# Turning the pack-attention weights in 32x32 blocks and through DRAM, from the third batch on

## The chip, the cores and the metric

The kernel runs on one core of a Trainium2 chip. The metric is device time in microseconds (us): 712.52 median of 3 runs (712.44 to 712.74). TensorE (PE) multiplies matrices into PSUM, its operands stand in SBUF; VectorE (DVE), ScalarE (ACT) and GpSimd (POOL) do elementwise work; SyncE (SP) issues nearly all DMA transfers. Each engine runs its own instructions in order and waits on semaphores for the others.

## The reference

Eight batches, each of 8 heads, 576 tokens, head width 64. For every batch and head a packed query set `p` (32 rows) attends to `k` and `v`; its result P serves as keys and values for `q`. The result, 4608 tokens by 512, goes through a feed-forward layer.

```python
p_packed = sm_attn(p, k, v)               # softmax(p k^T / 8) v : 32 x 64 per head
out = sm_attn(q, p_packed, p_packed)      # 576 x 64 per head
x = out.transpose(0, 2, 1, 3).reshape(B * S, H * D)
h = x @ w_in                              # 512 -> 2048
g = h * sigmoid(1.702 * h)
return g @ w_out                          # 2048 -> 512
```

Everything is float32. The two large products are made from pairs of rounded float32 parts (`hi` and `lo`), three products each.

## The kernel before, in words

For a batch `b` the second attention and `w_in` are folded together: M = P w_in (`m_chunk`, four column chunks of 512, parts `mhi` and `mlo` made by `m_upper` and `m_lower`), then h = A M (`h_mm`, 16 row blocks f of 128 by two token halves, 6 matmuls each), the gate (`h_tanh` on ACT, `h_gate` and `h_over` on DVE), its two parts (`h_upper`, `h_lower`), and the product with `w_out` (`out_mm`, 3 matmuls for each block f and each of four token groups, summed over f in four PSUM banks). The 64 tokens that don't fill a group of 128 are kept for two batches together and multiplied by `over_mm`.

The attention of batch b+1 is made in the middle of the feed-forward of batch b. Its first part: `scores1_mm` (two token halves; four heads of one parity stand in the 128 partitions, 32 rows of `p` each), `scores1_copy`, `scores1_max`, `bias1`, `exp1` (exponentials of one parity `eo`, a tile `x1` of 128x576), `sum1`. Then the weights have to be turned so that tokens are in the partitions: `turn1_mm` transposes four 128x128 pieces of `x1` on TensorE against the identity `ident` (line 340), once for each parity; `turn1_copy` brings the bank to the SBUF tile `aT` (lines 116, 118); `turn1_last_mm` and `turn1_last_copy` (lines 351, 359, 361) do the last 64 tokens, with a mask that zeroes the 64 that were done already. `pack` (line 373, 80 small matmuls) multiplies `aT` with `v`; `pack_end`, `pack_turn_mm`, `scores2_mm` and the second softmax (`max2` to `a_lower`) follow.

The order of all the work is written out by hand: `order` is a list of steps, run once, and each engine's instructions come in the order in which the list issues them. There is no other scheduler: what stands ahead in the list on the same engine goes first. Tiles with the same tag share buffers in turn: tag `x` has 5 (each `x1`, `x2`, `xt` takes one), `kqv` has 2 for all of k, q and v, tags `mhi`/`mlo` have 2 (`MB`). DMA instructions stand in the list too (`load`, `store`, `over_store`) and go out on SP's queue in that order; a DMA that has to wait holds up those behind it.

Of the kernel before, what the change touches and what calls it, by code (L numbers as in the profile page):

```python
# [21 lines left out]
def kernel(  # L22
# [635 lines left out]
    def over_store(pair, k):  # L658
        at = (2 * pair + k + 1) * S - REST
        nc.sync.dma_start(out[at : at + REST, :], taken["over"][k * REST : (k + 1) * REST, :])  # L660
# [123 lines left out]
        (h_gate, 0, 15, 0), (h_gate, 0, 15, 1), (h_over, 0, 15), (turn2, 1, 1), (out_mm, 0, 13, 3),
        (out_mm, 0, 14, 3), (out_mm, 0, 13, 2), (out_mm, 0, 14, 2), (a_upper, 1, 0, None),
        (a_lower, 1, 0, dve), (h_mm, 1, 0, 0), (h_upper, 0, 15, 0), (out_mm, 0, 13, 0),
        (upper_w, 31), (lower_w, 31, dve), (a_upper, 1, 1, None), (a_lower, 1, 1),
# [21 lines left out]
        (h_lower, 1, 2, 1), (out_mm, 1, 2, 2), (h_mm, 1, 5, 0), (out_mm, 1, 3, 2),
        (h_tanh, 1, 5, 0), (h_gate, 1, 5, 0), (out_mm, 1, 2, 0), (m_chunk, 1, 2),  # L810
        (m_upper, 1, 2, 1, None), (scores1_mm, 2, 1, inner), (scores1_max, 2, 1, 1),
        (scores1_max, 2, 1, 0), (bias1, 2, 0), (h_upper, 1, 4, 1, dve), (h_lower, 1, 4, 1, dve),
        (bias1, 2, 1), (scores1_copy, 2, 1, 0), (out_mm, 1, 2, 3), (exp1, 2, 0), (sum1, 2, 0),
        (out_mm, 1, 3, 1), (m_upper, 1, 2, 0, None), (m_lower, 1, 2, 0), (h_upper, 1, 5, 0, dve),
# [10 lines left out]
        (load, "q", 2, 1), (h_lower, 1, 7, 1), (h_lower, 1, 6, 1), (sum1, 2, 1), (out_mm, 1, 6, 1),
        (out_mm, 1, 6, 2), (h_over, 1, 6), (out_mm, 1, 5, 0), (h_mm, 1, 8, 0), (h_tanh, 1, 8, 0),
        (h_gate, 1, 8, 0), (h_upper, 1, 8, 0), (h_lower, 1, 8, 0), (h_mm, 1, 8, 1),
        (h_tanh, 1, 8, 1), (h_over, 1, 8), (store, 0, 2), (h_gate, 1, 8, 1), (h_upper, 1, 8, 1),
        (h_lower, 1, 8, 1), (turn1_copy, 2, 0), (out_mm, 1, 6, 3), (out_mm, 1, 7, 3),
        (out_mm, 1, 6, 0), (h_lower, 1, 7, 0, dve), (h_mm, 1, 10, 0), (out_mm, 1, 7, 0),  # L830
        (h_tanh, 1, 10, 0), (out_mm, 1, 8, 3), (turn1_last_mm, 2), (turn1_last_copy, 2),
        (h_mm, 1, 9, 0), (pack, 2), (h_tanh, 1, 9, 0), (out_mm, 1, 7, 1), (out_mm, 1, 8, 1),
        (pack_end, 2), (h_gate, 1, 10, 0), (h_gate, 1, 9, 0), (h_upper, 1, 9, 0, dve),
        (pack_turn_mm, 2), (out_mm, 1, 7, 2), (pack_turn_copy, 2), (scores2_mm, 2, 0, inner),
        (scores2_turn, 2, 0, 0), (m_chunk, 1, 3), (scores2_turn, 2, 0, 1),
        (h_upper, 1, 10, 0, dve), (max2, 2, 0), (m_upper, 1, 3, 0, None, dve), (h_mm, 1, 10, 1),
# [6 lines left out]
        (out_mm, 1, 9, 3), (m_upper, 1, 3, 1, None), (m_lower, 1, 3, 1), (h_upper, 1, 10, 1),
        (h_upper, 1, 11, 0, dve), (out_mm, 1, 9, 2), (h_lower, 1, 10, 1), (out_mm, 1, 10, 3),
        (h_tanh, 1, 11, 1), (sum2, 2, 0), (h_gate, 1, 11, 1), (h_upper, 1, 11, 1),
        (h_lower, 1, 11, 0), (out_mm, 1, 11, 1), (h_mm, 1, 12, 0), (h_over, 1, 11),
        (h_tanh, 1, 12, 0), (h_mm, 1, 12, 1), (h_tanh, 1, 12, 1), (h_gate, 1, 12, 0),
# [538 lines left out]
```

## Time and profile before

| what | value |
|---|---|
| median of 3 runs | 712.52 us (712.44 to 712.74) |
| the profiled execution | 712.61 us, span 710.8 us |
| PE busy | 697.2 us, 98% |
| DVE, ACT, POOL busy | 404.7, 277.6, 144.6 us |
| `pst` transposes (line 340) | 64 |
| `pstl` transposes (line 351) | 16 |

The span is the time from the first to the last instruction of the profiled execution; the 1.8 us between 710.8 and 712.61 lie around it. Busy times of matmuls overlap (a matmul is 0.3 to 0.6 us long from its start to its end, and the next starts before that), so what a matmul costs TensorE is read from a stretch of them: its length by the number of matmuls in it.

### The profile page before, as it was taken

Reading aid. Unit: us, or ns where it says so; the run is one execution under the profiler, and the core shown is the slowest. Engines: PE = TensorE matmul, PEld = TensorE weight load, DVE = VectorE, ACT = ScalarE, POOL = GpSimd, SP = SyncE. Lnnn points to the kernel's source line nnn. Section 1 sums busy time; section 2 is a strip of 40 time slices with the busy share of each in tenths; the row PEclk is TensorE's granted clock in tenths of the full one; section 3 lists DMA queues with packets and bytes.
Section 4 is the critical chain, followed back from the end, with each engine's and each line's share of the span. In section 5 each row is a group of like instructions: output and inputs, shape, how many; then the busy total and the mean of one; then the engine's idle time right before and its main releaser. Section 6 shows DMA issues by size and latency. Waiting matters only on the chain.

```text
span 710.8 us, 12972 instructions
## 1 busy us (share of the span) xinstructions
PE 697.2 (98%) x5092; PEld 568.2 (80%) x5092; DVE 404.7 (57%) x1027; ACT 277.6 (39%) x668; POOL 144.6 (20%) x172
## 2 busy tenths in 40 slices
PE   7899999999999999999999999999999999999997
PEld 5677788788888888888787788878787887878885
DVE  3988885437563466335635457643774556855543
ACT  4778544423323344454322433332342343333330
POOL 1553342123502223222332212202100000000000
PEclk9999999999999999999999999999999999999999
DMA  9886503310213103021110500313111020010001
GB/s 342 321 328 226 191 1 137 96 39 1 89 41 98 38 22 141 28 85 53 60 60 1 167 1 1 104 34 121 34 63 45 4 88 1 0 60 1 1 16 59
DMA packets 17404, 56.92 MB, mean 80 GB/s; under 512 B 1984, under 2 KB 3008, under 8 KB 16320
## 3 DMA queue, kind: packets, MB, share of 16 engines
q1 hardware_dynamic: 17344, 56.10, 22.2%
q8 instruction: 40, 0.66, 0.4%
q14 instruction: 20, 0.16, 0.1%
HBM read 46.65 MB, written 9.44 MB: 79 GB/s over the span
## 4 chain that ended last, share of the span: by engine, by line
PE 94%; DVE 3%; ACT 1%; DMA 1%; issue 0%; POOL 0%; SPq 0%; DVEq 0%; ACTq 0%; POOLq 0%
PE acc L624 49%; PE h L564 28%; PE acc_over L624 6%; PE psm_None L402 4%; PE ps L247 1%; PE ps L454 1%; PE pspv L373 1%; PE pst L340 1%; DMA k<-pk 1%; DVE x L465 0%; PE warm L124 0%; DVE w_in L217 0%; DVE wo L229 0%; ACT top L205 0%; DVE mx L485 0%
## 5 line engine op out<-in xcount | busy, mean ns | idle before, releaser
L624 PE MATMUL acc<-wo,ghi 128*128 128x512 f32 x1024 | 324.1, 398 | 0.0
L624 PEld LDWEIGHTS acc<-wo,ghi 128*128 128x128 f32 x1024 | 179.6, 188 | 39.0 <-issue 12.8
L624 PE MATMUL acc<-wo,glo 128*128 128x512 f32 x512 | 202.6, 396 | 0.3 <-POOL glo L551 0.2
L572 ACT ACTIVATE g<-h 128x288 f32<-128x288 f32 x256 | 103.9, 410 | 239.9 <-PE h L564 225.0
L554 DVE SCALAR_TENSOR_TENSOR g<-g,h 128x288 f32<-128x288 f32 (+1 forms) x256 | 105.7, 417 | 153.8 <-ACT g L572 152.8
L551 POOL TENSOR_TENSOR glo<-g,ghi 128x288 fp32r<-128x288 f32 (+1 forms) x119 | 89.7, 764 | 309.6 <-ACT ghi L116 199.9
L564 PE MATMUL h<-ahi,mhi 128*128 128x288 f32 x512 | 145.8, 300 | 1.1 <-DVE g L554 0.6
L564 PE MATMUL h<-ahi,mlo 128*128 128x288 f32 x512 | 143.5, 295 | 0.0
L624 PEld LDWEIGHTS acc<-wo,glo 128*128 128x128 f32 x512 | 96.2, 188 | 24.5 <-POOL glo L551 1.6
L564 PEld LDWEIGHTS h<-ahi,mhi 128*128 128x128 f32 x512 | 96.3, 188 | 19.9 <-DVE x L465 5.4
L564 PE MATMUL h<-alo,mhi 128*128 128x288 f32 x512 | 108.9, 294 | 0.0
L564 PEld LDWEIGHTS h<-ahi,mlo 128*128 128x128 f32 x512 | 96.5, 188 | 6.8
L116 ACT CAST ghi<-g 128x288 fp32r<-128x288 f32 (+1 forms) x161 | 63.3, 406 | 60.4 <-DVE g L554 39.3
L564 PEld LDWEIGHTS h<-alo,mhi 128*128 128x128 f32 x512 | 82.3, 188 | 0.2 <-POOL alo L533 0.2
L551 DVE TENSOR_TENSOR glo<-g,ghi 128x288 fp32r<-128x288 f32 (+1 forms) x137 | 60.5, 451 | 19.2 <-ACT ghi L116 15.9
L554 DVE SCALAR_TENSOR_TENSOR over<-g,h 128x64 f32<-128x64 f32 x128 | 27.4, 216 | 35.1 <-ACT g L572 34.8
L430 DVE TENSOR_TENSOR mlo<-psm_None,mhi 128x512 fp32r<-128x512 f32 x62 | 42.2, 684 | 5.9 <-ACT mhi L116 5.5
L624 PE MATMUL acc_over<-wo,ghi_over 128*128 128x512 f32 x128 | 39.9, 392 | 0.0
L116 ACT CAST mhi<-psm_None 128x512 fp32r<-128x512 f32 x44 | 25.7, 586 | 33.3 <-PE psm_None L402 33.3
L402 PE MATMUL psm_None<-w_in,PT 64*32 64x512 f32 x496 | 34.3, 596 | 0.0
L118 DVE CAST ghi<-g 128x224 fp32r<-128x224 f32 (+1 forms) x95 | 30.2, 324 | 5.6 <-PE acc L624 2.4
L624 PEld LDWEIGHTS acc_over<-wo,ghi_over 128*128 128x128 f32 x128 | 23.7, 188 | 4.8
(88 smaller groups left out, 492.9 us busy)
## 6 DMA issues: line engine op xcount, KB each, us to landing
q<-q SPq DMA_DIRECT2D x16, 576.0 KB, 5.6
v<-v SPq DMA_DIRECT2D x8, 1024.0 KB, 5.5
o<-o SPq DMA_DIRECT2D x32, 256.0 KB, 2.4
raw<-w_out SPq DMA_DIRECT2D x16, 511.8 KB, 7.4
raw<-w_in SPq DMA_DIRECT2D x12, 511.8 KB, 9.1
k<-pk SPq DMA_DIRECT2D x8, 640.0 KB, 4.0
k<-pk SPq DMA_DIRECT2D x8, 576.0 KB, 5.3
v<-v_last SPq DMA_DIRECT2D x8, 256.0 KB, 6.2
```

Of the source, the lines that this page charges most:

```text
L116: nc.scalar.copy(dst, src)
L118: engine.tensor_copy(dst, src)
L247: nc.tensor.matmul(bank[32 * j : 32 * j + 32, :NH], kq["p", b][rows(eo), j, :], kq["k", b][rows(eo), half, j, :], start=True, stop=True,)
L340: nc.tensor.transpose(bank[:, cs], st["x", 1, b, eo][:, cs], ident)
L373: nc.tensor.matmul(bank[32 * j : 32 * j + 32, e * D : (e + 1) * D], aT[:, c, e, 32 * j : 32 * j + 32], vt[:, c, e0 : e0 + D], start=(c == ...
L402: nc.tensor.matmul(banks[eo][32 * j : 32 * j + 32, columns(part)], PT[rows(eo), j, :], w_in_sb[fc][rows(eo), j, columns(part)], start=True ...
L430: nc.vector.tensor_tensor(lo, bank[:, at], hi.bitcast(F32), op=ALU.subtract)
L551: engine.tensor_tensor(lo, src, hi.bitcast(F32), op=ALU.subtract)
L554: nc.vector.scalar_tensor_tensor(dst, th, 1.0, h, op0=ALU.add, op1=ALU.mult)
L564: nc.tensor.matmul(h[:, :NH], m[eo][part][:, fo : fo + P], a[:, eo * NH : (eo + 1) * NH], start=(n == 0), stop=(n == len(terms) - 1),)
L572: nc.scalar.activation(g, st["h", b, f, half][:, :NH], AF.Tanh, scale=1.702)
L624: nc.tensor.matmul(acc, gp[:, at : at + P], wo[f][:, part, :], start=(start and i == 0), stop=(stop and i == 2),)
```

## The change

Batches 0 and 1 keep the old way. From batch 2 on, `turn1_mm`, `turn1_copy`, `turn1_last_mm` and `turn1_last_copy` are gone from the list: 12, 12, 6 and 6 steps. For each of these six batches there are instead 2 `turn1_blocks` (one VectorE transpose by 32x32 blocks, SBUF to SBUF, into a tile of tag `x`), 8 `turn1_out` (32 partitions of that tile to a DRAM tile `aside`, in runs of 32 floats) and 6 `turn1_in` (from DRAM to 32 partitions of `aT`, in runs of 256 floats). `aT` becomes one tile that stays, so the rows that the mask zeroed in batch 1 stay zero. Chunk 2 of M in the last batch gets a place of its own, in the buffer that `tops` had at the start. The last `over_store` is issued from ACT. The list is written anew from about the end of batch 0; apart from the steps named, the same steps stand in it, some of the elementwise ones on another engine.

```diff
+    LATE = [(B - 1, 2)]
-    tops = [cst.tile([P, DM], U32, name=f"top{i}") for i in range(4)]
+    tops = wk.tile([P, 4, DM], U32, tag="late", name="tops")
+    tops = [tops[:, i, :] for i in range(4)]
+    aT = cst.tile([P, KC, 2, P], F32, name="aT")
     def turn1_mm(b, eo):
-        if eo == 0:
-            st["aT", b] = wk.tile([P, KC, 2, P], F32, tag="aT", name=f"aT_{b}")
...
+    dram = ctx.enter_context(tc.tile_pool(name="dram", bufs=1, space=bass.MemoryType.DRAM))
+    NQ = P // NPK
+
+    def turn1_blocks(b, eo):
+        st["b", b, eo] = t = x_tile(f"xb_{b}_{eo}")
+        nc.vector.transpose(t, st["x", 1, b, eo])
+
+    def turn1_out(b, eo, j):
+
+        if ("aside", b) not in st:
+            st["aside", b] = dram.tile([NPK, S // NPK * 2 * P], F32, name=f"aside_{b}")
+        d = st["aside", b].rearrange("t (g i n) -> t g i n", i=2 * NP, n=NPK)
+        src = st["b", b, eo][NPK * j : NPK * (j + 1), :]
+        nc.sync.dma_start(d[:, :, NP * eo + j, :], src.rearrange("t (g n) -> t g n", n=NPK))
+
+    def turn1_in(b, i):
+
+        d = st["aside", b].rearrange("t (g i) -> t g i", i=2 * P)
+        n = (KC - 1) * NQ
+        if i < NQ:
+            at, c, src = NPK * i, slice(0, KC - 1), d[:, i:n:NQ, :]
+        else:
+            g = n + i - NQ
+            at, c, src = P - KLAST + NPK * (i - NQ), slice(KC - 1, KC), d[:, g : g + 1, :]
+        dst = aT[at : at + NPK, c].rearrange("t c e n -> t c (e n)")
+        nc.sync.dma_start(dst, src)
...
     def m_upper(b, fc, eo, part=None, engine=nc.scalar):
-        if not part:
+        if not part and (b, fc) in LATE:
+            if ("late", b, fc) not in st:
+                st["late", b, fc] = wk.tile(
+                    [P, 2, 2, FC], F32R, tag="late", name=f"late_{b}_{fc}"
+                )
+            st["m", b, fc, eo] = [st["late", b, fc][:, eo, i, :] for i in range(2)]
+        elif not part:
...
-    def over_store(pair, k):
+    def over_store(pair, k, engine=nc.sync):
```

The list around the new steps of batch 3, and its end:

```diff
+        (scores1_mm, 3, 1, inner), (scores1_copy, 3, 1, 0), (out_mm, 2, 3, 1), (out_mm, 2, 4, 1),
+        (m_upper, 2, 2, 0, None), (h_upper, 2, 4, 1), (out_mm, 2, 5, 1), (scores1_max, 3, 1, 0),
+        (bias1, 3, 0), (scores1_max, 3, 1, 1), (h_lower, 2, 5, 1, dve), (m_lower, 2, 2, 0),
+        (bias1, 3, 1), (exp1, 3, 0), (h_mm, 2, 6, 1), (turn1_blocks, 3, 0), (turn1_out, 3, 0, 0),
+        (scores1_copy, 3, 1, 1), (h_mm, 2, 6, 0), (h_lower, 2, 4, 1), (out_mm, 2, 3, 3),
+        (out_mm, 2, 4, 3), (turn1_out, 3, 0, 2), (exp1, 3, 1), (turn1_blocks, 3, 1),
+        (out_mm, 2, 4, 2), (h_tanh, 2, 6, 0), (turn1_out, 3, 1, 2), (h_tanh, 2, 6, 1),
+        (h_over, 2, 6), (h_gate, 2, 6, 0), (h_upper, 2, 6, 0), (h_lower, 2, 6, 0),
+        (turn1_out, 3, 1, 0), (turn1_out, 3, 0, 3), (turn1_out, 3, 1, 1), (h_gate, 2, 6, 1),
+        (h_upper, 2, 6, 1, dve), (h_lower, 2, 6, 1), (turn1_out, 3, 0, 1), (turn1_out, 3, 1, 3),
+        (h_mm, 2, 7, 0), (out_mm, 2, 5, 2), (h_tanh, 2, 7, 0), (h_gate, 2, 7, 0), (turn1_in, 3, 0),
+        (h_upper, 2, 7, 0), (m_upper, 2, 2, 1, None, dve), (turn1_in, 3, 2), (turn1_in, 3, 1),
+        (turn1_in, 3, 3), (h_mm, 2, 7, 1), (h_tanh, 2, 7, 1), (sum1, 3, 1), (h_gate, 2, 7, 1),
+        (out_mm, 2, 5, 3), (out_mm, 2, 6, 3), (h_upper, 2, 7, 1), (out_mm, 2, 6, 1),
+        (m_lower, 2, 2, 1), (h_mm, 2, 8, 0), (turn1_in, 3, 5), (out_mm, 2, 5, 0),
+        (out_mm, 2, 6, 0), (h_tanh, 2, 8, 0), (h_gate, 2, 8, 0), (turn1_in, 3, 4), (h_over, 2, 7),
+        (sum1, 3, 0), (h_lower, 2, 7, 1), (out_mm, 2, 7, 3), (h_lower, 2, 7, 0), (out_mm, 2, 7, 1),
+        (h_mm, 2, 8, 1), (h_tanh, 2, 8, 1), (h_gate, 2, 8, 1), (out_mm, 2, 7, 0), (h_over, 2, 8),
+        (pack, 3), (pack_end, 3), (h_upper, 2, 8, 0), (h_lower, 2, 8, 0, dve), (h_upper, 2, 8, 1),
...
+        (over_take, 3, dve), (over_store, 3, 1), (over_store, 3, 0, act),
```

## Rows read from the trace of the kernel before

**Rows 1.** The page: busy time by engine, 40 slices, DMA packets.
```profile
PE 697.2 (98%) x5092; PEld 568.2 (80%) x5092; DVE 404.7 (57%) x1027; ACT 277.6 (39%) x668; POOL 144.6 (20%) x172
PE   7899999999999999999999999999999999999997
PEclk9999999999999999999999999999999999999999
...
DMA packets 17404, 56.92 MB, mean 80 GB/s; under 512 B 1984, under 2 KB 3008, under 8 KB 16320
```

**Rows 2.** Busy time in four stretches: length, PE, PEld, DVE, ACT, POOL, clock, DMA.
```profile
0.00:28.00 28.00, 21.42 (x253) 15.27 (x259) 16.30 (x46) 14.29 (x36) 9.64 (x20) 1.00 0.95 368
28.00:128.00 100.00, 98.91 (x739) 79.62 (x730) 75.72 (x173) 62.37 (x141) 39.47 (x38) 1.00 0.46 172
128.00:253.00 125.00, 125.00 (x963) 102.32 (x963) 63.40 (x168) 42.69 (x108) 29.96 (x35) 1.00 0.18 57
253.00:710.80 457.80, 451.88 (x3147) 370.99 (x3145) 249.23 (x642) 158.23 (x385) 65.57 (x80) 1.00 0.14 49
```

**Rows 3.** The chain of waits, 128 to 180 us: start, length, what.
```profile
139.59 0.44 PE pst L340 x4
140.03 2.08 PE acc L624 x9
142.12 0.43 PE pst L340 x4
...
144.63 1.57 PE h L564 x12
...
150.46 0.22 PE pstl L351 x2
...
169.19 1.02 PE psm_None L402 x16
```

**Rows 4.** Groups of instructions by line: count, busy us, mean ns, idle before.
```profile
L116 ACT CAST ghi<-g 128x288 fp32r<-128x288 f32 (+1 forms) x161 | 63.3, 406 | 60.4 <-DVE g L554 39.3 <-PE acc L624 16.8 <-PE acc_over L624 3.2
...
L116 ACT CAST mhi<-psm_None 128x512 fp32r<-128x512 f32 x44 | 25.7, 586 | 33.3 <-PE psm_None L402 33.3
...
L205 ACT CAST top<-raw 128x512 f16<-128x512 bf16 (+1 forms) x36 | 24.5, 717 | 0.7 <-DMA raw<-w_out 0.6 <-DVE dec L217 0.2
...
L510 DVE STREAM_TRANSPOSE xt<-x 128x576 f32<-128x576 f32 (+1 forms) x17 | 12.4, 732 | 1.8 <-POOL x L504 1.7
...
L316 ACT ACTIVATE x<-x,nb 128x576 f32<-128x576 f32 x14 | 10.9, 776 | 3.4 <-DVE nb L300 3.2
L340 PE MATMUL pst<-ident,x 128*128 128x128 f32 x64 | 10.0, 284 | 0.0
...
L116 ACT COPY x<-ps 128x288 f32<-128x288 f32 x21 | 8.3, 399 | 10.9 <-DVE mx L292 7.9 <-PE ps L247 3.0
...
L118 DVE COPY aT<-pst 128x512 f32<-128x512 f32 x4 | 2.7, 687 | 2.6 <-PE pst L340 2.6
...
L316 ACT ACTIVATION_READ_ACCUMULATOR x<-x,nb 128x1 f32 x14 | 2.7, 190 | 0.0
```

**Rows 5.** What TensorE waited for: us, times, longest.
```profile
PE pspv L373 <- ACT aT L359: 0.3, 1, 0.3
```

**Rows 6.** SP's instructions in order of time: start, length, count.
```profile
625.97 1.41 SPq L644 DMA_DIRECT2D o<-o  x3
706.85 1.11 SPq L660 DMA_DIRECT2D o<-o_over  x2
```

**Rows 7.** DMA from 691 to 694 us: packets, share of 16 engines, KB, us to landing.
```profile
q1 hardware_dynamic: 144, 0.26, 23.3%
o<-o SPq DMA_DIRECT2D x1, 256.0 KB, 2.0
```

**Rows 8.** DMA from 240 to 244 us, the same columns.
```profile
q1 hardware_dynamic: 144, 0.66, 51.6%
k<-pk SPq DMA_DIRECT2D x1, 640.0 KB, 3.8
```

**Rows 9.** DMA from 705 to 711 us, the same columns.
```profile
o<-o_over SPq DMA_DIRECT2D x2, 128.0 KB, 2.3
```

**Rows 10.** The chain of waits from 694 us: start, length, what.
```profile
694.95 11.10 PE acc_over L624 x48
...
706.13 0.69 DVE o_over L118
```

More of the change, by code (lines that the diff above doesn't have):

```diff
@@ L784 @@
[L784 to L787, printed above, removed]
+        (h_lower, 0, 14, 1), (h_lower, 0, 13, 1), (out_mm, 0, 12, 1), (exp2, 1, 1),
+        (out_mm, 0, 13, 1), (turn2, 1, 0), (sum2, 1, 1), (norm2, 1, 1, None, pool),
@@ L809 @@
[L809 to L814, printed above, removed]
@@ new lines @@
+        (h_mm, 1, 5, 0), (out_mm, 1, 3, 2), (h_tanh, 1, 5, 0), (h_gate, 1, 5, 0),
+        (out_mm, 1, 2, 0), (m_chunk, 1, 2), (m_upper, 1, 2, 1, None), (scores1_mm, 2, 1, inner),
+        (scores1_max, 2, 1, 1), (scores1_max, 2, 1, 0), (bias1, 2, 0), (h_upper, 1, 4, 1, dve),
+        (h_lower, 1, 4, 1, dve), (bias1, 2, 1), (scores1_copy, 2, 1, 0), (out_mm, 1, 2, 3),
+        (exp1, 2, 0), (turn1_blocks, 2, 0), (sum1, 2, 0), (out_mm, 1, 2, 1), (out_mm, 1, 3, 1),
+        (m_upper, 1, 2, 0, None), (turn1_out, 2, 0, 0), (m_lower, 1, 2, 0), (turn1_out, 2, 0, 1),
@@ L825 @@
[L825 to L836, printed above, removed]
@@ L843 @@
[L843 to L847, printed above, removed]
-        (h_over, 1, 12), (out_mm, 1, 10, 2), (m_chunk, 2, 0), (h_upper, 1, 12, 0),
@@ new lines @@
+        (over_mm, 0, 3), (h_over, 2, 2), (h_gate, 2, 2, 1), (h_lower, 2, 1, 0, dve),
+        (h_mm, 2, 2, 0), (h_tanh, 2, 2, 0), (h_gate, 2, 2, 0), (h_mm, 2, 1, 1), (out_mm, 2, 0, 2),
+        (h_tanh, 2, 1, 1), (h_upper, 2, 2, 0, dve), (h_over, 2, 1), (h_gate, 2, 1, 1),
+        (h_upper, 2, 1, 1), (h_lower, 2, 1, 1), (h_upper, 2, 2, 1, dve), (m_chunk, 2, 1),
+        (m_upper, 2, 1, 0, None), (over_take, 0, dve), (scores1_mm, 3, 0, inner),
+        (h_lower, 2, 2, 1, dve), (scores1_copy, 3, 0, 1, dve), (scores1_max, 3, 0, 1),
@@ new lines @@
+        (out_mm, 4, 2, 1), (out_mm, 4, 2, 2), (scores1_mm, 5, 1, inner), (scores1_max, 5, 1, 0),
+        (scores1_copy, 5, 1, 0), (load, "q", 5, 0), (m_chunk, 4, 2), (h_upper, 4, 4, 1),
+        (bias1, 5, 0), (exp1, 5, 0), (h_mm, 4, 5, 1), (h_upper, 4, 3, 1, dve), (h_lower, 4, 3, 1),
+        (turn1_blocks, 5, 0), (turn1_out, 5, 0, 3), (turn1_out, 5, 0, 2), (h_tanh, 4, 5, 1),
+        (scores1_max, 5, 1, 1), (bias1, 5, 1), (turn1_out, 5, 0, 1), (h_over, 4, 5),
+        (m_upper, 4, 2, 0, None), (m_lower, 4, 2, 0), (scores1_copy, 5, 1, 1), (exp1, 5, 1),
@@ new lines @@
+        (h_gate, 5, 3, 0), (h_mm, 5, 4, 1), (h_upper, 5, 3, 0, dve), (h_lower, 5, 3, 0, dve),
+        (h_tanh, 5, 4, 1), (h_over, 5, 4), (h_gate, 5, 4, 1), (h_upper, 5, 3, 1), (store, 4, 2),
+        (out_mm, 5, 1, 1), (h_lower, 5, 3, 1, dve), (h_mm, 5, 4, 0), (h_tanh, 5, 4, 0),
+        (h_gate, 5, 4, 0), (out_mm, 5, 1, 3), (h_upper, 5, 4, 0, dve), (h_upper, 5, 4, 1, dve),
+        (m_chunk, 5, 2), (m_upper, 5, 2, 1, None), (scores1_mm, 6, 1, inner),
+        (scores1_copy, 6, 1, 1), (scores1_copy, 6, 1, 0, dve), (scores1_max, 6, 1, 0),
@@ new lines @@
+        (turn1_in, 6, 1), (turn1_in, 6, 0), (turn1_in, 6, 3), (turn1_in, 6, 5), (pack, 6),
+        (pack_end, 6), (out_mm, 5, 8, 1), (pack_turn_mm, 6), (pack_turn_copy, 6, dve),
+        (out_mm, 5, 7, 0), (scores2_mm, 6, 0, inner), (scores2_turn, 6, 0, 0), (m_chunk, 5, 3),
+        (m_upper, 5, 3, 0, None), (h_mm, 5, 10, 0), (h_tanh, 5, 10, 0), (m_upper, 5, 3, 1, None),
+        (scores2_turn, 6, 0, 1), (max2, 6, 0), (sub2, 6, 0, None), (h_gate, 5, 10, 0),
+        (h_upper, 5, 10, 0, dve), (h_lower, 5, 10, 0, dve), (h_mm, 5, 9, 1), (h_tanh, 5, 9, 1),
@@ new lines @@
+        (h_lower, 5, 11, 0, dve), (h_upper, 5, 10, 1), (h_lower, 5, 10, 1, dve),
+        (h_gate, 5, 11, 1), (out_mm, 5, 9, 0), (out_mm, 5, 10, 2), (store, 4, 1),
+        (out_mm, 5, 10, 0), (sum2, 6, 0), (m_chunk, 6, 0), (m_upper, 6, 0, 0, None),
+        (load, "k", 7, 0), (scores2_mm, 6, 1, inner), (norm2, 6, 0, None), (out_mm, 5, 10, 3),
+        (scores2_turn, 6, 1, 0), (scores2_turn, 6, 1, 1), (h_mm, 5, 12, 0), (h_tanh, 5, 12, 0),
+        (h_upper, 5, 11, 1, dve), (h_lower, 5, 11, 1, dve), (out_mm, 5, 11, 2), (h_mm, 5, 12, 1),
@@ new lines @@
+        (h_lower, 6, 9, 0, dve), (h_tanh, 6, 9, 1), (h_over, 6, 9), (turn1_in, 7, 0), (pack, 7),
+        (pack_end, 7), (h_mm, 6, 10, 0), (store, 5, 2), (pack_turn_mm, 7), (load, "q", 7, 0),
+        (h_lower, 6, 8, 0, dve), (out_mm, 6, 7, 1), (out_mm, 6, 8, 1), (out_mm, 6, 7, 2),
+        (pack_turn_copy, 7, dve), (h_tanh, 6, 10, 0), (h_gate, 6, 10, 0), (h_gate, 6, 9, 1),
+        (h_upper, 6, 9, 1), (store, 5, 3), (scores2_mm, 7, 0, inner), (m_chunk, 6, 3),
+        (m_upper, 6, 3, 1, None), (scores2_turn, 7, 0, 0), (scores2_turn, 7, 0, 1), (max2, 7, 0),
```

1046 lines of the change are left out of this document (513 added, 533 removed).

## The prediction

> **What bounds the kernel now.** I read the page first: TensorE is busy for 98% of the span at a granted clock of full speed in every slice, which is the higher of its two levels, 2.4 GHz; VectorE stands at 57%, ScalarE at 39% [rows 1]. Then four stretches [rows 2]: from 128 to 253 us TensorE is busy for 125.00 of 125 us, from 253 to the end for 451.88 of 457.8. What is missing there is nearly all the tail: the last matmuls end at 694.95 + 11.10 = 706.05 us [rows 10], 4.75 us before the end, so 5.92 - 4.75 = 1.2 us of real idleness in 458. VectorE is busy for 249/458 = 54% there, the DMA engines for 14%. So from batch 2 on (its first scores come after 100 us) only two things move the end: what TensorE does, and new waits of TensorE. Its waits are small before, those of `pack` for `aT` 0.3 us [rows 5].
>
> **The change part by part**
>
> *Transposes leave TensorE.* The chain shows a group of four at 0.44 and 0.43 us and the two last ones at 0.22 us, with the neighbours at their usual pace on both sides (9 of `out_mm` in 2.08, 12 of `h_mm` in 1.57) [rows 3]. The mean of 284 ns of one [rows 4] counts the overlap and would be too much. Per batch 0.44 + 0.43 + 0.22 = 1.09 us; six batches: **-6.5 us**. Nothing hides them, since TensorE has no idle time there.
>
> *The block transposes.* 12 on VectorE, of the same 128x576 shape as the row at 732 ns [rows 4]: 8.8 us more, less 4 copies of 687 ns. Some 6 us net on an engine with 46% free: 0, hidden beside the matmuls. Behind such a block on VectorE stand gates and parts of g; by both lists the shortest stretch from an `h_mm` to an `out_mm` that uses it is 3 `out_mm` (2.1 us). Without that cover the price would be 12 x 0.73 = 8.8 us. ScalarE loses work only.
>
> *The way through DRAM.* Per batch 8 `turn1_out`, then 6 `turn1_in`, each issued by SP, at 1.41/3 = 0.47 us for one of three in a row [rows 6]. `turn1_in` has to wait until all eight have landed; behind it on SP stand loads of q and k and stores. I went through SP's part of the list: nothing ahead of the new steps waits for work later than `scores1` of the same batch. Of the loads behind them the tightest is the second half of q of batch 4: it now follows both loads of the next k, which wait for `pack`; 9 + 8 + 8 packets of some 0.21 us and 1.7 us of landing are 7 us, with 9.8 us of TensorE work from the end of `pack` to its use. Reuse of the 5 buffers of tag `x` has 17 us or more to spare everywhere. So one deadline counts for each batch: `aT` complete when TensorE comes to `pack`.
>
> For batch 3, the closest, the list has 15 `out_mm` (0.695 us each) and 6 `h_mm` (0.785 us) between the second `scores1_mm` and `pack`: 15.1 us. In that time:
> - ScalarE: copy 0.40, `m_upper` 0.59, `h_upper` 0.41, exp 0.78 + 0.19, copy 0.40, exp 0.97 = 3.7 us; then the second block transpose 0.73, with 0.5 for handing over (an estimate): 5.0 us [rows 4].
> - Six `turn1_out` still to go. One has 32 x 18 = 576 runs of 128 bytes, 36 for each of 16 DMA engines. No row has a run so short. A store of 256 KB has 144 packets in 23.3% of 16 engines in 3 us: 78 ns each [rows 7]; a load with 5 KB packets 51.6% x 16 x 4 / 144 = 229 ns [rows 8]. 2.5 times the bytes take 2.9 times as long, so there is no fixed part to see: by bytes 128 would take 5 ns, and at the other end as long as 2 KB, 78 ns. No row tells which end is nearer; I take the middle of the ratio, 20 ns. One `turn1_out` is then 36 x 20 = 0.72 us of all DMA engines, six 4.3 us (the issue, 0.47 each, hides in it).
> - What landing costs beyond packets: the store landed after 2.0 us, 9 packets an engine of 78 ns in it: 1.3 us [rows 7].
> - Six `turn1_in`: the last is issued 5 x 0.45 = 2.25 us after the first; the 640 KB load landed after 3.8 us, 9 x 229 ns = 2.1 in it, so 1.7 fixed [rows 8], and 8 packets of 1 KB add 0.3: 2.0 us.
>
> Sum: 5.0 + 0.4 + 4.3 + 1.3 + 2.25 + 2.0 = 15.25 against 15.1 us: **+0.1 us**. In the same way for the others, with o for the time of one `turn1_out`, n of them still to go from t on, and 5.95 us for the rest (0.4 + 1.3 + 2.25 + 2.0): a batch can bear o = (work up to `pack` - t - 5.95) / n. Batch 3: (15.1 - 5.0 - 5.95) / 6 = 0.7. Batch 5, with 16 `out_mm`, 5 `h_mm` and an `m_chunk` of 1.0: (16.1 - 5.4 - 5.95) / 5 = 0.95. Batch 4: (18.4 - 4.7 - 5.95) / 6 = 1.3. In 7, 2 and 6 all eight count: (20.3 - 3.6 - 5.95) / 8 = 1.35, (20.2 - 2.6 - 5.95) / 8 = 1.45, (23.1 - 2.8 - 5.95) / 8 = 1.8. Only batch 3 is at its limit with 0.72. At 5 ns no batch waits and the issue bounds: 0 us. At 78 ns, o = 2.8: 12.6 + 9.3 + 9.1 + 11.8 + 10.8 + 8.2 = 62 us of new waits.
>
> The Trainium skill, "DMA: Bandwidth & Descriptors" (section "Specifications"), speaks against this part: transfers need 512 B or more for line rate, and below that the DMA engine reads, modifies and writes. No packet of data in these rows is that small. What it would make of the time is the first rival.
>
> *The tail.* The last two stores are issued in 1.11 us, the second some 0.5 us after the first [rows 6], and each lands after 2.3 us [rows 9]. From ScalarE the second goes beside the first: **-0.5 us** (0 if the issue there is slower by as much). The 0.69 us of `over_take` stays [rows 10].
>
> *A third place for M, `tops` in one tile, the new list.* The third place lets `m_chunk` of the last batch come earlier; TensorE does the same work: 0. The new list can win at most the 1.2 us of idleness and the 1.1 us before 128 us; what it can lose isn't bounded by a row, beyond this: the distances from h to its product, and of the PSUM reuse behind it, are as short and as many as before. I take 0.
>
> Sum against the profiled execution: 712.6 - 6.5 - 0.5 + 0.1 = 705.7; two thirds of the 0.3 us that `pack` waited go as well: **705.5 us**. That execution lies 0.1 us above the median of the runs, less than can be told.
>
> **The rivals**
>
> *Small runs are slow (slower than before).* The mechanism is the one above: each 128-byte run into DRAM costs much more than its bytes. `pack` of every batch then stops TensorE until the last `turn1_in` has landed. It takes back the 7 us at o = 1.38 us, or 38 ns a run: 6 x 0.68 + 5 x 0.43 + 6 x 0.09 + small rests = 7 us. At 50 ns (o = 1.8) the waits sum to 6.5 + 4.3 + 3.1 + 3.7 + 2.7 = 20 us: 726 us; at 78 ns 767. For it: of 17,404 packets only 1984 are under 512 B, 16 for each of the 124 transfers and none of them data [rows 1], so nothing shows the price of a short run. Against it: no fixed part from 2 KB to 5 KB. Chance 0.15. By the rule of the Trainium skill named above a run would be read and written, twice its bytes, 10 ns, and nothing would wait; the page gives no price for it.
>
> *Part is given back.* Two or three `pack`s wait 1 to 2 us each (o near 1.1), or the new list has stops of that sum, or the four parts of `tops`, now one tile, make each of 36 conversions (0.72 us, [rows 4]) wait for the join before it in the first 90 us. 2 to 5 us come back: 708 to 711. For it: SP, the transfers and two engines now stand in a row ahead of `pack`. Chance 0.15.
>
> *Nothing is gained.* If the transposes filled time that TensorE would have waited anyway, for gates or for VectorE, the list would just move the wait: 712. Against it: a full 125 of 125 us [rows 2]. Chance 0.07.
>
> *More is gained*, by the idleness that the new list can take: 704.2. Chance 0.03.
>
> **How the numbers follow.** Forecast 705.5 with its own range 704.6 to 708, chance 0.60. About 0.2% (1.4 us) is what a measurement here can tell from no change. Faster: 0.60 + 0.15 + 0.03 = 0.78. Same: 0.07. Slower: 0.15. The range has the forecast, what is given back and no gain: 704.6 to 713.5; it leaves out some 0.18, the slow runs above and the larger gain below.
>
> **What would show it.** Lines 340 and 351 with 16 and 4 matmuls; TensorE busy about 690 us; the chain still over 94% TensorE. On the row of `pack` the wait for a DMA of `aT`: under 1 us in all by the forecast, over 7 us by the first rival, largest in batch 3. The page's packets under 512 B, 27,648 of them new (48 x 576), with a duration that decides between 5, 20 and 78 ns. The last two stores side by side. Wrong it would be if TensorE waited for something else in sum, VectorE's gates above all, or if a `turn1_out` lands much later than 2.0 us after its issue.

## The result, and the profile after

The changed kernel takes 704.57 us (median of 4, 703.91 to 706.67) against 712.48 before (712.23 to 712.74): ratio 0.9897 with a 95% interval of [0.9885, 0.991] (so in every ratio below), 7.9 us less. The profiled execution took 703.91 us with a span of 702.1; before it was 712.61 and 710.8. Forecast were 705.5 us and a gain of 7.1.

The page of the changed kernel, busy time and slices, answers to [rows 1]:

```profile
PE 688.1 (98%) x5032; PEld 561.8 (80%) x5032; DVE 434.5 (62%) x1099; ACT 259.9 (37%) x621; POOL 121.8 (17%) x141
PE   7899999999999999999999999999999999999997
PEclk9999999999999999999999999999999999999999
DMA packets 49853, 64.01 MB, mean 91 GB/s; under 512 B 30976, under 2 KB 35456, under 8 KB 48768
```

TensorE has exactly 60 matmuls less (5092 - 5032), the 10 transposes of six batches, at the same clock and still at 98%. Packets under 512 B rose by 30,976 - 1984 = 28,992: the 27,648 expected, and 1344 more, 16 for each of the 84 new transfers.

The last two of the four stretches in [rows 2] (length, PE, PEld, DVE, ACT, POOL, clock, DMA):

```profile
128.00:253.00 125.00, 124.08 (x942) 101.94 (x923) 68.23 (x174) 42.50 (x106) 30.03 (x35) 1.00 0.29 82
253.00:702.10 449.10, 443.91 (x3099) 365.40 (x3097) 274.32 (x707) 140.68 (x340) 42.66 (x49) 1.00 0.20 58
```

The stretch that was full before, 128 to 253 us, now lacks 0.92 us; behind it 449.10 - 443.91 = 5.2 us are missing, 4.33 of them the tail behind the last matmul. The groups by line (343 and 354 are the transposes that are left, 374 the block transposes, 406 `pack`; count, busy us, mean ns, idle before) and the list of TensorE's waits (us, times, longest) name it:

```profile
L343 PE MATMUL pst<-ident,x 128*128 128x128 f32 x16 | 2.7, 280 | 0.7 <-ACT x L312 0.7
L354 PE MATMUL pstl<-ident,x 128*128 128x128 f32 x4 | 0.8, 286 | 0.0
L374 DVE STREAM_TRANSPOSE xb<-x 128x576 f32<-128x576 f32 x12 | 9.1, 770 | 5.1 <-ACT x L319 5.0
L406 PE MATMUL pspv<-v,aT 128*32 128x64 f32 x640 | 11.1, 221 | 1.3 <-DMA aT<-aside 0.9 <-ACT aT L362 0.3
```

```profile
PE pspv L406 <- DMA aT<-aside: 0.9, 1, 0.9
PE h L603 <- DVE g L593: 0.6, 1, 0.6
PE acc L663 <- DVE glo L590: 0.5, 1, 0.5
```

One `pack` waits once, and no other does: it is that of batch 3, as the chain of waits from its scores to it shows (start, length, what):

```profile
220.72 0.59 PE ps L250 x16
221.31 0.39 ACT x L117
...
224.27 0.88 ACT x L319 x2
...
225.17 0.78 DVE xb L374
...
228.91 0.63 SPq L382
...
229.58 3.51 DMA aside<-xb
...
234.64 2.76 DMA aT<-aside
...
237.50 1.39 PE pspv L406 x80
```

This is the forecast's row of steps: ScalarE's exp, the second block transpose, SP issuing, the last `turn1_out` landing, SP issuing the `turn1_in`, landing, `pack`. The link that is too long is the 3.51 us of the last `turn1_out`, from its issue to its landing, for which 2.0 were forecast. What one of them costs, from SP's instructions and from DMA in a quiet stretch (batch 7, 559 to 568 us; for a queue packets, MB, share of 16 engines, for an issue KB and us to landing):

```profile
224.89 5.32 SPq L382 DMA_DIRECT2D aside<-xb  x8
```

```profile
q1 hardware_dynamic: 4753, 0.61, 43.4%
aside<-xb SPq DMA_DIRECT2D x8, 72.0 KB, 2.3
```

SP's pitch is 5.32/8 = 0.67 us, and a packet takes 43.4% x 16 x 9 us / 4753 = 13 ns, so a `turn1_out` is 36 x 13 = 0.47 us of the DMA engines: the issue on SP sets the pace, not the transfer.

### The profile page after: what moved, and what is told of

It is laid out like the page before. It is cut to its first block, busy times and chain, and to the rows that moved or that the text cites. A ratio compares the mean times of both kernels' runs of the same rounds, so it can differ in the third digit from the quotient of the medians.

```text
span 702.1 us, 13011 instructions
## 1 busy us (share of the span) xinstructions
PE 688.1 (98%) x5032; PEld 561.8 (80%) x5032; DVE 434.5 (62%) x1099; ACT 259.9 (37%) x621; POOL 121.8 (17%) x141
## 2 busy tenths in 40 slices
DMA packets 49853, 64.01 MB, mean 91 GB/s; under 512 B 30976, under 2 KB 35456, under 8 KB 48768
## 4 chain that ended last, share of the span: by engine, by line
PE 91%; DVE 4%; DMA 2%; issue 1%; ACT 1%; SPq 1%; DVEq 0%; ACTq 0%
PE acc L663 48%; PE h L603 28%; PE acc_over L663 5%; PE psm_None L435 4%; PE ps L493 1%; PE ps L250 1%; PE pspv L406 1%; DMA k<-pk 1%; DMA aside<-xb 0%; DVE mlo L469 0%; DMA aT<-aside 0%; PE warm L125 0%; SPq L382 0%; DVE glo L590 0%; DVE wo L232 0%
## 5 line engine op out<-in xcount | busy, mean ns | idle before, releaser
L603 PE MATMUL h<-ahi,mhi 128*128 128x288 f32 x496 | 140.3, 298 | 1.1 <-DVE g L593 0.6
L603 PE MATMUL h<-ahi,mlo 128*128 128x288 f32 x496 | 138.9, 295 | 0.0
L590 POOL TENSOR_TENSOR glo<-g,ghi 128x288 fp32r<-128x288 f32 (+1 forms) x88 | 67.7, 777 | 243.7 <-ACT ghi L117 115.5
L603 PEld LDWEIGHTS h<-ahi,mhi 128*128 128x128 f32 x496 | 93.2, 188 | 18.9 <-DVE x L504 5.7
L603 PE MATMUL h<-alo,mhi 128*128 128x288 f32 x496 | 105.4, 294 | 0.0
L603 PEld LDWEIGHTS h<-ahi,mlo 128*128 128x128 f32 x496 | 93.3, 188 | 6.9
L590 DVE TENSOR_TENSOR glo<-g,ghi 128x224 fp32r<-128x224 f32 (+1 forms) x168 | 73.9, 452 | 21.0 <-ACT ghi L117 17.5
L603 PEld LDWEIGHTS h<-alo,mhi 128*128 128x128 f32 x496 | 79.6, 188 | 0.2 <-POOL alo L572 0.2
L117 ACT CAST ghi<-g 128x288 fp32r<-128x288 f32 (+1 forms) x135 | 53.2, 405 | 45.8 <-DVE g L593 35.8
L119 DVE CAST ghi<-g 128x288 fp32r<-128x288 f32 (+1 forms) x121 | 36.3, 308 | 6.8 <-PE acc L663 1.4
```

The lines of the kernel that those rows point to most:

```text
L117: nc.scalar.copy(dst, src)
L119: engine.tensor_copy(dst, src)
L590: engine.tensor_tensor(lo, src, hi.bitcast(F32), op=ALU.subtract)
L603: nc.tensor.matmul(h[:, :NH], m[eo][part][:, fo : fo + P], a[:, eo * NH : (eo + 1) * NH], start=(n == 0), stop=(n == len(terms) - 1),)
```

## The experiments

Each has a median of 4 to 11 executions, the kernel before (712.1 to 712.5 us) measured beside it.

**The changed kernel again**, without an edit.

> The changed kernel once more, nothing edited: 704.6 us by both theories. Open is its spread (703.91 to 706.67 in four executions). Theory 1: it is the wait of `pack` of batch 3, of 0.93 us in the one profile seen, where the last `turn1_out` landed 1.3 us later than its neighbours while a 16 KB instruction fetch held one DMA engine; then a new profile shows another wait there (0 to 2 us), and the rest of the gaps of TensorE as before. Rival: the spread lies elsewhere, and the wait of that `pack` is again 0.9.

704.22 us (703.96 to 704.41), ratio 0.9887 [0.9874, 0.9901]. The wait of batch 3's `pack` is the same as in the first profile:

```profile
238.01 1.32 PE L406 MATMUL pspv<-v,aT 128*32 128x64 f32 x80 [0.94 <-DMA aT<-aside]
```

So theory 1 falls: this wait is steady and no cause of spread. The two profiles differ by 0.5 us in the first 28 us, where this one waits 1.0 us for `w_in` and the first didn't. Where 706.67 came from stays open.

**The transposes back on TensorE, in the new list.** For b = 2 to 7:

```
-        (turn1_blocks, b, 0), (turn1_blocks, b, 1),
-        (turn1_out, b, eo, j), (turn1_in, b, i),
+        (turn1_mm, b, 0), (turn1_copy, b, 0),
...
+        (turn1_mm, b, 1), (turn1_copy, b, 1, dve),
...
+        (turn1_last_mm, b), (turn1_last_copy, b),
...
         (pack, b),
```

> The new list with the transposes of batches 2 to 7 back on TensorE (2 x 4 and 2 per batch, 8, 5 and 2 steps of TensorE ahead of `pack`), without block transposes, `turn1_out`, `turn1_in`. The prediction's size of 1.09 us per batch gives 704.6 + 6.5 - 1.0 (the wait of batch 3's `pack` goes) = 710.1 us. The rival size, from the distances between the starts of TensorE's matmuls (0.36 + 0.36 + 0.135 = 0.86 per batch), gives 704.6 + 5.2 - 1.0 = 708.8; then the new list, and not the transposes, gave over 2 us. If the list gave nothing, it is 712.

710.74 us (710.13 to 711.47), ratio 0.998 [0.9971, 0.9989]. That is 6.5 us above the changed kernel, though the wait of batch 3's `pack` is gone. The edit made one wait of its own, for `pn` (0.5 of these; the other 1.1 us is batch 0's and stands in all kernels):

```profile
PE pspt L425 <- ACT pn L419: 1.6, 2, 1.1
```

The transposes are then worth 6.5 + 0.9 - 0.5 = 6.9 us, give or take some 0.6 by the spread of the executions (against the next run, which has neither way, 710.74 - 702.89 - 0.5 = 7.3): the prediction's 6.5 holds, and the rival size of 5.2 doesn't. By the distances between the starts of matmuls the groups themselves take 5.2 us, as the rival has it; but `out_mm`, by the same distances, takes 366.6 us in all here and 364.6 in the next run, so the matmuls around the groups lose 2.0 more. The rest of the way to the old kernel, 712.34 - 710.74 = 1.6 us, is the new list with the tail, without any transposes saved. One wait of the old list that is in no trace of the new one, from the list of waits of the kernel before (the scores of batch 5 wait for a gate, near 374 us):

```profile
PE ps L247 <- DVE g L554: 0.5, 1, 0.5
```

But in sum the waits of TensorE that the traces list behind 28 us are 2.0 us before and 2.1 here, and its idle time ahead of the end of the last matmul is 710.8 - 4.8 - 697.2 = 8.8 us before and 709.1 - 4.4 - 695.7 = 9.0 here. The list's gain is in the busy time, for the same number of matmuls; the page of this run:

```profile
PE 695.7 (98%) x5092; PEld 567.8 (80%) x5092; DVE 430.4 (61%) x1093; ACT 264.9 (37%) x633; POOL 122.0 (17%) x141
```

What makes it shorter stays open. The new list also gives 26 more `h_upper` and 31 more `h_lower` to VectorE, and no run takes that back by itself.

**Without the way through DRAM.**

```
-        (turn1_blocks, b, eo), (turn1_out, b, eo, j), (turn1_in, b, i),
```

> The changed kernel without `turn1_blocks`, `turn1_out` and `turn1_in` in batches 2 to 7 (`pack` there reads the transposed weights of batch 1, so this part of the computation is left out). If the way through DRAM costs TensorE nothing but the wait of batch 3's `pack`: 704.6 - 1.0 = 703.6 us. If the block transposes on VectorE, SP's longer queue or the transfers delay TensorE in other places too: under 703, with the wait of each such place gone from the trace.

702.89 us (702.56 to 703.95), ratio 0.9871 [0.9858, 0.9885], 1.3 us below the changed kernel. 0.9 of it is the wait of `pack`; the waits for g (0.6) and for `glo` (0.5) are those of the changed kernel, so they are the list's. The remaining 0.4 is within what the medians can tell. Twelve block transposes and 84 transfers cost TensorE nothing else.

**The old list with the way through DRAM put in place.** For b = 2 to 7, and `LATE = []`:

```
         (exp1, b, 0),
-        (turn1_mm, b, 0), (turn1_copy, b, 0), (turn1_mm, b, 1), (turn1_copy, b, 1),
-        (turn1_last_mm, b), (turn1_last_copy, b),
+        (turn1_blocks, b, 0), (turn1_out, b, 0, 0), (turn1_out, b, 0, 1),
+        (turn1_out, b, 0, 2), (turn1_out, b, 0, 3),
...
         (exp1, b, 1),
+        (turn1_blocks, b, 1), (turn1_out, b, 1, 0), (turn1_out, b, 1, 1),
+        (turn1_out, b, 1, 2), (turn1_out, b, 1, 3),
+        (turn1_in, b, 0), (turn1_in, b, 1), (turn1_in, b, 2),
+        (turn1_in, b, 3), (turn1_in, b, 4), (turn1_in, b, 5),
```

> The list of before with the way through DRAM put in the place of the transposes: block transpose and four `turn1_out` right behind each `exp1`, six `turn1_in` behind the last; nothing else moved, one place less for M, last store on SP. Theory: from the end of a batch's later exp to `pack` the way needs about 1.0 + 4 x 0.67 + 2.45 + 2.3 + 1.9 = 10 us (pitch of `turn1_out`, landing, six `turn1_in`, landing, as measured in the trace after), and the list of before gives less in batches 3, 4, 5 and 6: waits of 1.0, 1.8, 6.4 and 3.6 us, none in 2 and 7; 712.6 - 5.2 to 6.5 + 12.8 = 719 to 720 us, slower than before. Rival: the order is no matter, since loads and stores on SP have slack: 706 to 707 us with waits under 2 us in all.

728.82 us (725.46 to 729.9), ratio 1.0221 [1.0199, 1.0243]: slower than before. TensorE's waits, its `pack`s of batches 4 and 5, and granted clocks behind them (stretches as above):

```profile
PE pspv L406 <- DMA aT<-aside: 13.3, 4, 4.8
PE h L603 <- DVE g L593: 3.0, 3, 1.6
```

```profile
317.88 1.36 PE L406 MATMUL pspv<-v,aT 128*32 128x64 f32 x80 [2.48 <-DMA aT<-aside]
410.95 2.19 PE L406 MATMUL pspv<-v,aT 128*32 128x64 f32 x80 [4.80 <-DMA aT<-aside]
```

```profile
319.00:322.00 3.00, 3.00 (x22) 2.29 (x11) 0.00 (x0) 0.79 (x3) 0.66 (x1) 0.51 0.52 155
411.00:415.00 4.00, 4.00 (x87) 3.44 (x88) 0.00 (x0) 0.66 (x3) 0.00 (x0) 0.57 0.89 246
500.15:504.15 4.00, 4.00 (x87) 3.63 (x88) 0.00 (x0) 0.53 (x2) 0.00 (x0) 0.60 0.40 121
600.00:604.00 4.00, 3.78 (x103) 2.64 (x111) 0.00 (x0) 0.78 (x3) 0.00 (x0) 1.00 0.21 48
```

The sum of the waits was forecast well (12.8, measured 13.3), their places less so: 2.5, 4.8, 4.3 and 1.8 us in batches 4 to 7, none in 3. The time was missed by 9 us for two reasons that the forecast lacked. Block transposes that stand on VectorE until an exp ends hold up gates behind them: 3.0 us of waits for g instead of 0.6. The first of these, near 230 us, on VectorE:

```profile
228.80 0.78 DVE L374 STREAM_TRANSPOSE xb<-x 128x576 f32<-128x576 f32 x1 [2.00 <-ACT x L319]
```

And behind each of the three longest waits the granted clock is near half, 1.2 GHz, for some microseconds: 0.49 x 3 + 0.43 x 4 + 0.40 x 4 = 4.8 us lost. These make 7.2; some 2 us stay open. So the order is no side matter: the way through DRAM put in the place of the transposes costs 16 us in the old order and wins 6.5 in the new one (710.74 to 704.22). The 7.9 of the whole change have the new list's own gain in them.

**`pack` of batch 3 later.**

```
-        (pack, 3), (pack_end, 3),
...
         (h_mm, 2, 9, 1), (h_tanh, 2, 9, 1), (h_gate, 2, 9, 1), (h_over, 2, 9),
+        (out_mm, 2, 6, 2), (pack, 3), (pack_end, 3),
-        (pack_turn_mm, 3), (pack_turn_copy, 3), (out_mm, 2, 6, 2),
         (h_mm, 2, 9, 0),
...
         (h_lower, 2, 9, 0),
+        (pack_turn_mm, 3), (pack_turn_copy, 3),
```

> The changed kernel with `pack` of batch 3 one `h_mm` and one `out_mm` (0.785 + 0.695 = 1.48 us of TensorE's work) later in the list, everything else in its order. Theory: its wait of 1.0 us for `aT` is the way through DRAM being 1 us too long for the list, and nothing else hangs on it: 704.2 - 1.0 = 703.2 us, no wait of `pack` for a DMA left. Rival: the wait only moves on to `pack_turn` or to the second scores of batch 3, which come after it: 704.2.

703.38 us (702.92 to 703.71), ratio 0.9875 [0.9861, 0.9888]: 0.8 us less, and no wait of `pack` for a DMA in its trace. The wait was TensorE's own loss, and it doesn't come back.

**Long runs instead of short.**

```
-        d = st["aside", b].rearrange("t (g i n) -> t g i n", i=2 * NP, n=NPK)
         src = st["b", b, eo][NPK * j : NPK * (j + 1), :]
-        nc.sync.dma_start(d[:, :, NP * eo + j, :], src.rearrange("t (g n) -> t g n", n=NPK))
+        i = NP * eo + j
+        nc.sync.dma_start(st["aside", b][:, S * i : S * (i + 1)], src)
```

> Each `turn1_out` writes its 32 rows of 2304 bytes as they stand, in one run each, instead of 576 runs of 128 bytes (the order within P's weights is then another, so this part of the result is left out of the computation; bytes, waits and the list are the same). If short runs cost what the trace shows (a pitch of 0.67 us against 0.47 for one issue on SP, 13 ns a packet): the first `turn1_in` of batch 3 is issued some 6 x 0.2 = 1.2 us earlier, the wait of its `pack` is gone, 703.2 us, and no other batch changes. Rival: the wait comes from the landing alone (a 16 KB instruction fetch holds one DMA engine for 1.25 us): pitch and wait stay within 0.3 us of what they were, 704.2.

702.97 us (702.44 to 703.52), ratio 0.9872 [0.9857, 0.9887]; `pack` waits for no DMA. SP in batch 3:

```profile
224.43 3.74 SPq L382 DMA_DIRECT2D aside<-xb  x8
229.14 3.09 SPq L394 DMA_DIRECT2D aT<-aside  x6
```

Eight issues in 3.74 us instead of 5.32, a pitch of 0.47: the first theory has the pitch right. That the wait is gone has more than this one reason. The landing is shorter too (median 1.8 us for the eight, and 1.8 for the last, instead of 3.5), and the first `turn1_in` goes 1.4 us after the last `turn1_out` instead of 3.7, since with this order of bytes it needn't wait for all eight: the waits are not the same, as the expectation has it. So the 704.22 - 702.97 = 1.2 us are the most that 128-byte runs cost the kernel.

**No third place for M.**

```
-    LATE = [(B - 1, 2)]
+    LATE = []
...
-        (m_chunk, 7, 2, inner),
...
         (h_mm, 7, 3, 1), (h_tanh, 7, 3, 1), (h_over, 7, 3),
-        (m_chunk, 7, 3),
+        (m_chunk, 7, 2),
...
         (out_mm, 7, 5, 3),
+        (m_chunk, 7, 3),
```

> The changed kernel without the third place for M: the third `m_chunk` of the last batch and its parts go where the fourth stood (behind the last `h_mm` that reads the first part), the fourth behind the last that reads the second. The prediction took the third place for 0: 704.2 us, within 0.4. Rival: the 2 us that the new list won over the old one beside the transposes come from it: 705.5 or more, with new waits of TensorE between 610 and 650 us.

704.91 us (704.45 to 704.96), ratio 0.9895 [0.9882, 0.9909], 0.7 above the changed kernel. 0.4 of it is a wait for `w_in` in the first 28 us, where nothing was edited (1.4 us against 1.0 in the run above); 0.4 is a second wait for `glo`, near 648 us:

```profile
PE acc L663 <- DVE glo L590: 0.9, 2, 0.5
```

This lies between the two expectations (704.6 and 705.5). By these traces the third place is worth about 0.4 us; it isn't the new list's gain.

**Batch 1 through DRAM as well**, tried twice with `pack` of batch 3 later. In both tries batch 1's `turn1_mm`, `turn1_last_mm` and their copies go, and its second `exp1` moves up. The first time:

```
         (load_w, 21),
+        (turn1_out, 1, 0, 0), (turn1_out, 1, 0, 1), (turn1_out, 1, 0, 2), (turn1_out, 1, 0, 3),
...
         (load_w, 25),
+        (turn1_out, 1, 1, 0), (turn1_out, 1, 1, 1), (turn1_out, 1, 1, 2), (turn1_out, 1, 1, 3),
```

> `pack` of batch 3 later as in the run beside it, and batch 1 through DRAM too (its second exp moved up behind the first; blocks, `turn1_out`, `turn1_in` among the loads of the weights). Theory: 1.09 us of transposes less, and the way fits (from the end of its second exp, now near 56 us, 13 us to `pack` at 69.5): 704.2 - 1.0 - 1.1 = 702.1 us. Rival: in the stage where the weights are still being loaded and decoded, the transfers and the blocks delay the conversions, and TensorE waits for weights or for `aT`: 703.5 or more.

710.0 us (708.41 to 711.78), ratio 0.9969 [0.9956, 0.9981]. The rival: the loads of weights stand on SP behind eight `turn1_out`. The last of those shown goes out at 64.64 us, where with `pack` of batch 3 later alone it is 57.00; ScalarE waits 6.17 us for one, and TensorE 4.0 behind it:

```profile
58.81 2.89 SPq L382 DMA_DIRECT2D aside<-xb  x4
...
64.64 0.38 SPq L189 DMA_DIRECT2D raw<-w_out  x1
```

```profile
70.56 1.39 ACT L208 CAST tops<-raw 128x512 f16<-128x512 bf16 x2 [6.17 <-DMA raw<-w_out]
```

```profile
PE h L603 <- DVE over L593: 4.0, 1, 4.0
PE pspv L406 <- DMA aT<-aside: 1.9, 1, 1.9
```

The waits aren't all of it. Behind each of these two the granted clock is half, 1.2 GHz, while TensorE is at work for 3.04 and 3.80 us (stretches as above), which loses 3.4 us more:

```profile
72.70:75.74 3.04, 3.04 (x9) 2.22 (x9) 2.94 (x4) 3.04 (x8) 2.42 (x2) 0.50 0.99 161
77.60:81.40 3.80, 3.80 (x86) 3.63 (x87) 1.46 (x5) 1.46 (x4) 1.09 (x1) 0.50 0.32 102
```

The second time all eight went behind those loads:

```
         (load, "v", 1, 1),
+        (turn1_out, 1, 0, 0), (turn1_out, 1, 0, 1), (turn1_out, 1, 0, 2), (turn1_out, 1, 0, 3),
+        (turn1_out, 1, 1, 0), (turn1_out, 1, 1, 1), (turn1_out, 1, 1, 2), (turn1_out, 1, 1, 3),
```

> As the run with `pack` of batch 3 later and batch 1 through DRAM, which failed by loads of weights stuck behind eight `turn1_out` on SP (5.1 us on VectorE for a conversion, 4.0 us on TensorE behind it): now the second exp of batch 1 and both block transposes a few steps later, and all `turn1_out` behind the loads of weights and of v, only one load of weights and one of q after them. Theory: SP is free from 58 us on, the last `turn1_out` ends near 63 us, the last `turn1_in` lands near 69, `pack` comes near 69.5: 703.4 - 1.1 (transposes) - 0.3 (its wait for a copy) = 702.0 us. Rival: the way still ends late, or conversions wait again: 703.4 or more.

710.33 us (709.35 to 711.35), ratio 0.9975 [0.9964, 0.9985]. Now `pack` of batch 1 waits 5.9 us, and over the 4 us behind it the granted clock is 0.62. SP between 57 and 72 us:

```profile
57.58 9.09 SPq L382 DMA_DIRECT2D aside<-xb  x8
...
68.37 2.78 SPq L394 DMA_DIRECT2D aT<-aside  x6
```

Behind loads of weights and v the eight take 9.09 us, 1.14 each, not 5.4: the pitch is only 0.67 while the DMA engines have little else. Batch 6 of the changed kernel shows the same: 5.98 us for its last five, while two loads of q and two stores run. So the third batch is the first for which the way through DRAM pays in the orders tried.

**The last store back on SP.**

```
-        (over_store, 3, 0, act),
+        (over_store, 3, 0),
```

> The changed kernel with the second last store back on SP behind the other, nothing else. The prediction's term: 0.5 us longer from the last matmul to the end; by the traces it should be 4.75 us again instead of 4.34, and 704.6 us. Rival: the store from ScalarE is no sooner complete than one queued on SP, and the 0.4 us of difference between the two traces is chance: 4.3 us again, 704.2.

704.57 us (703.62 to 705.03), ratio 0.9894 [0.9879, 0.9909]. From the last matmul's end to the end of the span it is 4.54 us, against 4.33 with ScalarE and 4.76 before. Neither expectation: ScalarE's issue is worth some 0.2 us, and the two traces with SP differ by as much. The changed kernel's last transfers tell why (697 to 702.1 us):

```profile
o<-o_over SPq DMA_DIRECT2D x1, 128.0 KB, 2.3
o<-o_over ACTq DMA_DIRECT2D x1, 128.0 KB, 2.6
```

The half microsecond of queueing is saved, and 0.3 of it goes into a later landing.

**A better version**: `pack` of batch 3 later, and one `out_mm` ahead of each of the two other waits.

```
-        (h_mm, 0, 14, 0), (h_tanh, 0, 14, 0), (h_gate, 0, 14, 0), (out_mm, 0, 12, 2),
+        (out_mm, 0, 12, 2), (h_mm, 0, 14, 0), (h_tanh, 0, 14, 0), (h_gate, 0, 14, 0),
...
+        (out_mm, 2, 14, 2),
         (out_mm, 2, 15, 3),
...
-        (out_mm, 2, 14, 2),
```

> The changed kernel with `pack` of batch 3 later as in the run before, and two `out_mm` moved ahead of the waits of TensorE that the new list left or made: one ahead of the `h_mm` near 94 us that waits for a gate (0.76 us over its usual distance), one ahead of the `out_mm` near 274 us that waits for a part of g (0.68). Theory: such waits are lost time one by one, since nothing but TensorE sets the end: 704.2 - 0.8 - 0.7 - 0.7 = 702.0 us. Rival: each comes back as a wait a few steps on, for the same gate or part of g: 703.4 as with the later `pack` alone.

701.79 us (701.47 to 701.96), ratio 0.985 [0.9837, 0.9864]: faster than both kernels. What TensorE still waits for after 28 us, all of it:

```profile
PE pspv L406 <- ACT aT L362: 0.3, 1, 0.3
PE h L603 <- ACT x L117: 0.2, 1, 0.2
```

## Why the prediction was right, and where it was not

The forecast of 705.5 us lies 0.9 above the measured median and 1.6 above the profiled execution; the median, 704.57, stands at the lower end of the range given (704.6 to 713.5), and the run without an edit at 704.22. By its steps:

- *Transposes, -6.5.* Right: 6.9 by undoing it. Reading the pace from the chain [rows 3] was the right choice.
- *Block transposes on VectorE, 0.* Right: they took 9.1 us (8.8 forecast), and leaving them out with the transfers wins only the wait of `pack` and 0.4 that can't be told from nothing. The cover is the order: put in the old list, they held gates for over 2 us.
- *The way through DRAM, +0.1.* Right in mechanism, place (batch 3 alone) and pitch of `turn1_out` (0.72 forecast, 0.67 measured), mis-sized by 0.8: it cost 0.9. The pitch came out for another reason: a run costs 13 ns, below the 20 chosen, but each issue takes 0.67 on SP, which the forecast had hidden at 0.47. The term that failed is the landing. From the end of the second block transpose to the last `turn1_out` in DRAM were forecast 0.4 + 4.3 + 1.3 = 6.0 us; the chain has 233.09 - 225.95 = 7.1, and 1.5 of the 3.51 us of the last one is more than the 2.0 taken: 0.3 of that is in a landing in a quiet stretch too (2.3), 1.2 is batch 3's alone (see the end). The `turn1_in` came as forecast in sum, 237.41 - 233.09 = 4.3 us against 2.25 + 2.0, though not in parts: by the chain it is the fourth of the six that lets `pack` go, 2.76 us after its issue.
- *The tail, -0.5.* Half right: 0.2 by undoing it, 0.4 between the traces; a later landing on ScalarE's queue takes the rest.
- *Third place for M and the new list, 0.* Wrong: with the transposes on TensorE the new list with the tail is 1.6 us faster than the old one, in spite of a wait of its own of 0.5. Without that wait, and without the 0.2 of the tail, the list is worth 1.9. Some 0.4 is the third place, 0.5 the wait of the scores of batch 5 that is gone; for the other 1 us the record shows no place. The bound of 2.3 us that was given held as a number, but not by its reason: it was put on idle time, and the idle time stayed (8.8 us before, 9.0 with the new list), while the busy time fell.
- *Two thirds of the 0.3 us that `pack` waited.* Wrong: this wait is still there, near 70 us; it is batch 1's, which keeps its transposes.

In the order above the errors are -0.4, 0, +0.8, +0.3, -1.9 and +0.2 us, and they sum to -1.0: 8.1 us were gained against the kernel before beside the run without an edit (712.34 to 704.22), 7.1 forecast. That the number came within a microsecond is partly luck, since the list's error alone is almost twice that. The way and its place, batch 3, are not luck: they were worked out link by link, and the runs show them.

The number that came is that of the rival with the chance 0.03 (more is gained, 704.2), but its mechanism, idle time that the new list takes, is not what the traces show. The first rival (short runs slow) was decided by the packets: 13 ns where it needed 38. The trace of before had a closer row for it than those chosen: its 1984 packets under 512 B, 4 bytes each, take 9 ns (median). The Trainium skill, "DMA: Bandwidth & Descriptors" (section "Specifications"), wants 512 B or more for line rate. The trace agrees: by its share of a 2 KB packet of 78 ns [rows 7] a 128-byte one would take 5 ns, and it takes 13. The second rival (part given back) came in with one `pack` and less than 1 us; nothing of `tops` was seen in the waits.

What the profile was to show came, but for the chain: 91% TensorE where over 94 was forecast, as it follows the way through DRAM for batch 3, and that wait is one microsecond of 700. The sign of being wrong that was named, a `turn1_out` landing much later than 2.0 us, came as well: 3.5 to 4.3 us for the last three of batch 3, and a median of 4.9 for those of batch 6 (466 to 480 us), where there was time to spare and no `pack` waited.

## What to carry to other kernels

When the bounding engine is full, work taken off it pays in full only if the other way ends before the engine arrives, so draw up that way link by link for each place, with the landing of the last transfer taken from a busy stretch: the same substitution lost 16 us in one order and won 6.5 in another. A long way through DRAM belongs where its queue has nothing behind it that others wait for and where the DMA engines are free. Afterwards look at the waits that remain one by one: three small moves in the list won 2.4 us more.

## What the runs showed that was not expected

- After waits of TensorE of 2.5, 4.8 and 4.3 us the granted clock was 0.51, 0.57 and 0.60 over 3 to 4 us (behind the first of them only once `pack` had run), and `pack` took 2.19 us instead of 1.36. After 1.8 and after 0.9 us it stayed at 1.00. The tries with batch 1 show the same behind 4.0 and 5.9 us. A long wait costs more than its length.
- The last three `turn1_out` of batch 3 landed 4.3, 3.9 and 3.5 us after their issue where 2.3 is the median. In the last stretch (231.5 to 232.4 us) hardly any DMA engine works, 73 packets in 9.2% of 16 engines (the first row); the stretch from 229.5 to 233.4 has one packet of instructions, 2.0% x 16 x 3.9 = 1.25 us of one engine (the others):

```profile
q1 hardware_dynamic: 73, 0.01, 9.2%
```

```profile
q1 hardware_dynamic: 1776, 0.22, 37.6%
q8 instruction: 1, 0.02, 2.0%
aside<-xb SPq DMA_DIRECT2D x2, 72.0 KB, 3.7
```

In the four other traces with these steps of batch 3 in the same order (the run without an edit, `pack` later, no third place, last store on SP) there is one such packet between 227 and 233.5 us, and the last `turn1_out` lands after 3.5 to 3.7 us. That the fetch of instructions held one engine, which then had to finish its share alone, is read from these rows and not shown: no run moved the fetch alone.
